# Two mixtures of experts behind a short attention: side work queued behind residues, expert scales folded into factors, and a new rate for layer two's weights

## The chip, the core and the metric

The kernel runs on one core of a Trainium2 chip. The metric is the device time of one execution in microseconds (us). The engines are named as in the profile: PE multiplies matrices (PEld is its loading of weights), DVE and ACT work on whole tiles, POOL issues the gathers and scatters and some small operations, SP issues all other transfers. Each engine takes its instructions in the order of its queue, and an instruction that waits for a semaphore holds up all behind it.

## What is computed

There are N = 7168 tokens of D = 192 numbers. A causal local attention comes first (window K = 7, 8 heads, softmax over the window). Then layer one sends each token to its two best of E = 8 experts, layer two to its best one. An expert is `relu(x @ w1[e]) @ w2[e]` with 1024 hidden numbers.

```python
# layer one
noisy = x @ w_gate + log1p(exp(x @ w_noise)) * noise
top2 = argpartition(-noisy, 2)[:, :2]; g = softmax(noisy at top2)
out[t] = sum over k of g[t, k] * (relu(x[t] @ w1[e]) @ w2[e])      # e = top2[t, k]
# layer two, on the output x of layer one
logits = (x / (norm(x) + 1e-6)) @ (emb / (norm(emb) + 1e-6)).T / tau
out[t] = max(softmax(logits[t])) * (relu(x[t] @ w1[e]) @ w2[e])    # e = argmax
```

## The kernel before

**Tiles.** A list of rows is made for each layer: rows are sorted by expert into tiles of 256 (pairs) and, at the end of a layer's sections, of 128 (singles). Layer one has 56 pairs and 4 singles that always run, layer two 28 and 4; further singles stand in a branch that is seldom taken. The loop over `seq` runs one tile per turn: `first_product` of the next tile (line 1112: 40 products, in four groups; ACT makes the float16 part `hh` of each group, line 1114; DVE makes its residue, line 1115, called `hl` or `wt` by the buffer) is interleaved with `second_product` of this one (line 1138, 48 products), then ACT scales the result (line 1143) and POOL scatters it (line 1146): layer one's to `yb`, layer two's to the output. Rows come by gathers that POOL issues three tiles ahead (line 1062, into `xg`), weights by SP (line 1080, `wb<-ws`), one tile's in two transfers, skipped where the expert is still in the buffer.

**Scaling.** Values are kept as two float16 parts, with powers of two taken out. A row's factor travels with it in column 192 of `xg`; that of an expert is in `cprod`. For each tile DVE multiplies the two into `sc` (line 1123), which ACT applies at line 1143. `scales` (line 742) looks up `cprod` for each place in the order of tiles, into `csl`.

**Side work.** All that makes the lists is done beside the tiles: the attention of token columns 24 to 40 and 40 to 56 (the first 24 come in the head, where no tile runs yet), its logits, choices, ranks and lists s1 and s2 (lists two and three of layer one); then for layer two `combine_gen` (loads `yb`, adds a token's two results with the choice factors `gates`), `post_chunk` (norms, splitting and logits of four columns, a chunk), `choose2`, `gate_gen` (the factor of each row, and the rows themselves), ranks and lists c0, c1, c2; and `prep_gen`, which reads an expert's weights, takes their power of two out, splits them into two float16 parts (`wo`, ACT line 366 and DVE line 368) and writes them to `ws`. Layer one's weights are done in the head, layer two's beside the tiles: eight jobs, 56 pieces at line 368.

These are Python generators that yield their cost in us on DVE (real part) or ACT (imaginary part). `Queue.point` runs at eight points of a pair's turn, six of a single's, and hands out `SHARE` = 0.845 us of credit on each. It runs steps of threads and chains while credit is left, and `P_STEPS` = 0.64 steps of the weights' thread a point. Before the gather of the first tile of a new list, `finish` runs all steps that are left for that list. `yield "lag"` in a generator leaves it until the next point.

**The order.** What a generator emits gets the next priority in the tile framework; the framework's scheduler orders each engine's queue by priority among what it takes to be ready. So an instruction of side work can stand in DVE's queue ahead of a residue that was emitted before it. `tc.issue_after(x.ins)` puts an instruction behind x in the queue of x's engine. `after_product` does so with the last product on PE and is used for side work there; `after_tile` does so with the last residue on DVE (`state["pin"]`) and is used for the taps of the attention alone (line 420).

Of the kernel before, what the change touches and what calls it, by code (L numbers as in the profile page):

```python
# [7 lines left out]
F32 = mybir.dt.float32  # L8
F16 = mybir.dt.float16
BF16 = mybir.dt.bfloat16  # L10
I32 = mybir.dt.int32
AF = mybir.ActivationFunctionType
# [4 lines left out]
NCOL = N // 128  # L17
# [12 lines left out]
R_LOW = 40000  # L30
P_STEPS = 0.64
SHARE = 0.845
# [51 lines left out]
def two_moe(ctx: ExitStack, tc: tile.TileContext, x, wgen, w_gate, w_noise, noise, w1a, w2a, emb, tau, w1b, w2b, out):  # L84
# [35 lines left out]
    def lag(n):  # L120

        for _ in range(0 if head["on"] else n):
            yield "lag"
# [264 lines left out]
    def softmax_gen(a, b):  # L388
        n = (b - a) * H
        w = wt[:, a:b].rearrange("p t h k -> p (t h) k")  # L390
        m = rt.tile([128, GM * H], F32, name="sm_m")
        with (tc.issue_after(state["ctl"].ins) if a == G1[1][0] else ExitStack()):
            V.tensor_reduce(m[:, :n], w, axis=AX.X, op=ALU.max)
        yield 6.0e-3 * n
        V.tensor_tensor(w, w, m[:, :n, None].to_broadcast([128, n, K]), op=ALU.subtract)
        yield 6.0e-3 * n
        A.activation(w, w, AF.Exp)
        yield 0.5
        V.tensor_reduce(m[:, :n], w, axis=AX.X, op=ALU.add)
        V.tensor_scalar(m[:, :n], m[:, :n], 1e-9, None, op0=ALU.add)  # L400
        V.reciprocal(m[:, :n], m[:, :n])
        yield 12.0e-3 * n
        V.tensor_mul(w, w, m[:, :n, None].to_broadcast([128, n, K]))
        yield 6.0e-3 * n
# [48 lines left out]
    sx = consts.tile([128, 2, NCOL], F32, name="sx")  # L453
    isx = consts.tile([128, 2, NCOL], F32, name="isx")
    y_loads = []

    def post_chunk(l, acc, a, lg, g0, rows_i, done, whole=None):
# [5 lines left out]
        for c in range(CH):  # L463
            A.activation(rows_i.bitcast(F16)[:, c, 0:192] if l else xs[:, c], acc[c], AF.Square, accum_out=nrm[:, l, a + c:a + c + 1])
        yield 1.6j
        pow2(nrm[:, l, s].bitcast(I32), sx[:, l, s], isx[:, l, s], CH, 194, 60)
        yield 0.4
# [113 lines left out]
    def gate_gen(g, lg, a, b):  # L581

        n = b - a
        s = rt.tile([128, GM], F32, name="ss")[:, :n]
        with tc.issue_after(state["lg"].ins) if "lg" in state else ExitStack():
            PL.tensor_tensor(s, nrm[:, 1, a:b], half[:, :n], op=ALU.pow)
        yield 0.1
        yield from lag(4)
        V.tensor_scalar(s, s, 1e-6, None, op0=ALU.add)
        V.reciprocal(s, s)  # L590
        V.tensor_scalar(s, s, itau[:, 0:1], None, op0=ALU.mult)
        V.tensor_mul(lg, lg, s[:, :, None].to_broadcast([128, n, E]))
        yield 0.8
        A.activation(lg, lg, AF.Exp)
        yield 0.4
        yield from lag(1)
        V.tensor_reduce(s, lg, axis=AX.X, op=ALU.add)
        V.tensor_scalar(s, s, 1e-9, None, op0=ALU.add)
        V.reciprocal(s, s)
        V.tensor_mul(gate2[:, a:b], s, isx[:, 1, a:b])  # L600
        yield 0.7
        V.tensor_copy(rows2[g][:, :, 192:196].bitcast(F32), gate2[:, a:b, None].to_broadcast([128, b - a, 4]))
        write_rows(1, rows2[g], a, b - a)
        yield 0.2
# [62 lines left out]
    flag_i = [consts.tile([128, len(L.order)], I32, name=f"fi{l}") for l, L in enumerate((L1, L2))]  # L667
    csl = [consts.tile([128, len(L.order)], F32, name=f"csl{l}") for l, L in enumerate((L1, L2))]
    gidx = [consts.tile([128, L.units], I32, name=f"gx{l}") for l, L in enumerate((L1, L2))]
# [71 lines left out]

    def scales(l, a, b):
        while l not in ready:
            yield None
        n = b - a
        e = exec_e[l]
        t = rt.tile([128, 768], F32, name="cmp")[:, 0:64 * E].rearrange("p (a b) -> p a b", b=E)
        V.tensor_tensor(t[:, :n], e[:, a:b, None].to_broadcast([128, n, E]), iof[:, None, 0:8].to_broadcast([128, n, E]),
                        op=ALU.is_equal)
        yield 0.6  # L750
        V.tensor_mul(t[:, :n], t[:, :n], cprod[l][:, None, :].to_broadcast([128, n, E]))
        V.tensor_reduce(csl[l][:, a:b], t[:, :n], axis=AX.X, op=ALU.add)
        yield 0.9

# [85 lines left out]
    def decode(l, v, n, us):  # L840
# [10 lines left out]
        else:  # L851
            vi = rt.tile([128, 128], F32, name="df2").bitcast(I32)
            pv = rt.tile([128, 128], I32, name="dpv")
            V.tensor_copy(vi[:, :n], v)
# [29 lines left out]
    def section_open(l, L, g, key):  # L884
# [32 lines left out]
        def tables():  # L917
            yield from slot_experts(l, s0, s1)
            yield from exec_tables(l, s0, s1)
            yield from scales(l, s0, s1)  # L920

# [37 lines left out]
    def section_last(l, L, key):  # L959
# [30 lines left out]
        def tables():  # L990
# [22 lines left out]
            yield from exec_tables(l, sec, len(L.order))  # L1013
            yield from scales(l, sec, len(L.order))

# [39 lines left out]
    def gather(i):  # L1055
        l, L, pos, u, nh = tiles[i]

        xg = att.tile([128, 1, RW], I32, name="junk", bufs=1) if "rare" in state else work.tile([128, 2, RW], I32, name="xg", bufs=4)
        rows_in = 128 * L.groups[max(g for g in range(len(L.groups)) if pos >= L.first[g])][1]
        live[i] = {"xg": xg}  # L1060
        for h in range(nh):
            PL.indirect_dma_start(out=xg[:, h], out_offset=None, in_=T[l][0:rows_in],  # L1062
                                      in_offset=bass.IndirectOffsetOnAxis(ap=gidx[l][:, u + h:u + h + 1], axis=0))
# [33 lines left out]
    def first_product(i, bg):  # L1097
# [7 lines left out]
        for g in range(4):  # L1105
# [14 lines left out]
            yield  # L1120
        xg = live[i]["xg"]
        sc = work.tile([128, 2], F32, name="sc1", bufs=1) if "rare" in state else work.tile([128, 2], F32, name="sc", bufs=3)
        V.tensor_scalar(sc[:, :nh], xg[:, :nh, 192:193].bitcast(F32).rearrange("p h o -> p (h o)"), csl[l][:, c:c + 1], None, op0=ALU.mult)  # L1123
        live[i] = {"h": (hh, hl), "sc": sc}

    def second_product(i, bg):
        l, L, pos, u, nh = tiles[i]
        _, w = slot(i)
        (hh, hl), sc = live[i]["h"], live[i]["sc"]
        w2 = w[:, 4096:].rearrange("p (f a d) -> p f a d", f=8, a=2)  # L1130
# [11 lines left out]
        for h in range(nh):  # L1142
            A.activation(ys[:, h], py[:, h], AF.Copy, scale=sc[:, h:h + 1])  # L1143
        dst, bound = (YB, 2 * N - 1) if l == 0 else (out, N - 1)
# [38 lines left out]
    def combine_gen(g):  # L1183
        a, b = L2.groups[g]
        while state.get("free", 0) < 1 if g == 0 else 1 not in ready:
            yield None
        nxt = combine_load(a)
        yield from lag(5)
        for c0 in range(a, b, CH):
# [30 lines left out]
    def ctl(l, g, key):  # L1220
# [4 lines left out]
        if l == 0:  # L1225
            yield from choose1(lgs[0][g], a, b)
        else:
            yield from choose2(lgs[1][g], a, b)
            bgq.chain(gate_gen(g, lgs[1][g], a, b), key)
# [4 lines left out]
    class Job:  # L1234
# [4 lines left out]

        def step(self):  # L1240
            if self.rank is None:
                return next(self.g)
# [8 lines left out]
    class Queue:  # L1251
# [29 lines left out]
        def point(self, share):  # L1281
# [5 lines left out]
            for it in list(self.chains):  # L1287
                if min(self.credit.real, self.credit.imag) < -0.6:
                    break
                try:  # L1290
# [8 lines left out]
                    moved = True  # L1299
            self.steps += P_STEPS  # L1300
            while self.steps >= 1.0:
# [153 lines left out]
```

## Time and profile before

| | us |
|---|---|
| median of three runs (1038.93 to 1042.97) | 1039.67 |
| profiled execution | 1037.56 |
| its span, first to last instruction | 1035.8 |

| engine | busy us | share | instructions |
|---|---|---|---|
| PE | 907.2 | 88% | 9714 |
| DVE | 698.4 | 67% | 1852 |
| ACT | 579.9 | 56% | 1247 |
| POOL | 396.5 | 38% | 368 |

The profile is of one execution. Busy shares mix the head (to 145 us, without tiles), the stretch with attention and layer one, the change of layers, and the end, where tiles run without side work; a stretch's limit is read from that stretch. The views used below are the table of busy time by stretch, the chain that ended last in order of time, the waits of an engine by what ended them, single instructions in order of time, and the instructions of one line.

### The profile page before, as it was taken

The numbers are of one execution on the slowest core, as the hardware profiler recorded it, in microseconds if no ns is written. First come the engines' busy times: TensorE is split into PE (matmuls) and PEld (weight loads), VectorE is DVE, ScalarE is ACT, GpSimd is POOL, SyncE is SP. The second block draws the span as 40 slices with busy tenths as digits, with TensorE's granted clock in tenths as the row PEclk, the third lists the DMA queues.
The fourth block names the chain that finished last, engine by engine and source line by source line (L and its number), as shares of the span: only waits on it lengthen the run. The fifth ranks groups of instructions, "written<-read, shape, count | busy, mean of one in ns | idle before, by whom it ended". The sixth has DMA issues, their size and how long they took to land.

```text
span 1035.8 us, 26302 instructions
## 1 busy us (share of the span) xinstructions
PE 907.2 (88%) x9714; PEld 824.9 (80%) x9714; DVE 698.4 (67%) x1852; ACT 579.9 (56%) x1247; POOL 396.5 (38%) x368
## 2 busy tenths in 40 slices
PE   4894159999998899799998989879998999999995
PEld 2452138988897798699997879869988999999995
DVE  7897988999998788965357667385757763333331
ACT  2879635567565767455565854265447444444442
POOL 1000053565245453316443535344435354444422
PEclk9997569999999999999998989999999999999998
DMA  8687873766469486546989959674576835777650
GB/s 270 194 271 228 294 271 107 255 185 198 132 213 348 156 265 229 167 178 209 323 312 334 358 196 320 207 250 147 182 260 215 295 121 185 262 262 265 220 219 22
DMA packets 96395, 236.34 MB, mean 228 GB/s; under 512 B 13439, under 2 KB 64223, under 8 KB 87808
## 3 DMA queue, kind: packets, MB, share of 16 engines
q1 hardware_dynamic: 79360, 200.35, 56.7%
q0 software_dynamic: 16896, 34.20, 10.8%
q8 instruction: 79, 1.29, 0.5%
q14 instruction: 60, 0.49, 0.1%
HBM read 230.60 MB, written 57.90 MB: 279 GB/s over the span
## 4 chain that ended last, share of the span: by engine, by line
PE 51%; DVE 21%; DMA 10%; issue 6%; ACT 6%; POOL 3%; SPq 1%; POOLq 0%; DVEq 0%; ACTq 0%
PE ph L1112 23%; PE py L1138 20%; DVE tmp L420 3%; DMA wb<-ws 3%; PE py L447 2%; DVE wo L368 2%; DVE hl L1115 2%; DVE wt L1115 2%; DVE acc L435 2%; DMA xg<-t,gx 2%; DMA tmp<-yb 2%; PE pt L1090 2%; ACT wo L366 1%; PE rb L503 1%; POOL xg L1062 1%
## 5 line engine op out<-in xcount | busy, mean ns | idle before, releaser
L1112 PE MATMUL ph<-xt,wb 128*128 128x256 f16 x3360 | 421.8, 278 | 37.8 <-DVE hl L1115 17.0
L1112 PEld LDWEIGHTS <-wb 128*128 128x128 f16 x3360 | 330.4, 100 | 81.9 <-issue 27.8
L1138 PE MATMUL py<-wb,hh 128*128 128x192 f16 x2688 | 354.9, 247 | 0.0
L1114 ACT ACTIVATE hh<-ph 128x512 f16<-128x512 f32 (+1 forms) x368 | 210.3, 577 | 232.3 <-PE ph L1112 218.1
L1062 POOL DMA_INDIRECT xg<-t,gx x176 | 191.3, 1087 | 343.6 <-DVE gx L849 133.0
L1138 PEld LDWEIGHTS <-hh 128*128 128x128 f16 x2816 | 253.9, 98 | 3.8
L1146 POOL DMA_INDIRECT yb<-ys,sx x116 | 128.6, 1109 | 186.8 <-ACT ys L1143 161.2
L1115 DVE SCALAR_TENSOR_TENSOR wt<-ph,hh 128x512 f16<-128x512 f32 x184 | 125.9, 687 | 100.3 <-ACT hh L1114 100.0
L1138 PE MATMUL py<-wb,wt 128*128 128x192 f16 x736 | 181.5, 247 | 0.0
L1115 DVE SCALAR_TENSOR_TENSOR hl<-ph,hh 128x512 f16<-128x512 f32 (+1 forms) x184 | 117.4, 641 | 84.1 <-ACT hh L1114 81.8
L1138 PE MATMUL py<-wb,hl 128*128 128x192 f16 x608 | 149.8, 246 | 0.0
L1143 ACT ACTIVATE ys<-py,sc 128x192 f32<-128x192 f32 x176 | 64.6, 416 | 89.5 <-PE py L1138 76.5
L1146 POOL DMA_INDIRECT out_dram<-ys,sx x60 | 61.3, 1021 | 94.0 <-ACT ys L1143 80.0
L420 DVE TENSOR_TENSOR tmp<-xh,wt 128x768 f32<-128x768 f32 x90 | 84.5, 950 | 2.9 <-PE ph L447 1.5
L1138 PEld LDWEIGHTS <-wt 128*128 128x128 f16 x736 | 72.2, 98 | 0.1
L1092 ACT ACTIVATE xt<-pt 128x768 f16<-128x768 f16 x84 | 67.9, 808 | 4.4 <-PE pt L1090 4.3
L1138 PEld LDWEIGHTS <-hl 128*128 128x128 f16 x672 | 66.1, 98 | 0.1
L1123 DVE TENSOR_SCALAR sc<-xg,csl 128x2 f32<-128x2 f32 (+1 forms) x92 | 21.2, 233 | 57.7 <-ACT ys L1143 53.0
L366 ACT ACTIVATE wo<-xh,wsc 128x384 f16<-128x384 f32 (+1 forms) x76 | 45.9, 659 | 16.0 <-DVE wsc L261 15.8
L1090 PE MATMUL pt<-identh,xg 128*128 128x128 f16 x528 | 45.8, 222 | 8.4 <-DMA xg<-t,gx 8.4
L368 DVE SCALAR_TENSOR_TENSOR wo<-xh,wsc,wo 128x384 f16<-128x384 f32 (+1 forms) x76 | 48.9, 675 | 3.3 <-ACT wo L366 3.2
L447 PE MATMUL py<-tmp,ident 128*128 128x384 f32 x84 | 33.9, 554 | 15.2 <-DVE tmp L420 13.7
(323 smaller groups left out, 990.2 us busy)
## 6 DMA issues: line engine op xcount, KB each, us to landing
wb<-ws SPq DMA_DIRECT2D x84, 1024.0 KB
wb<-ws SPq DMA_DIRECT2D x84, 768.0 KB
ws<-wo SPq DMA_DIRECT2D x16, 768.0 KB
tmp<-yb SPq DMA_DIRECT2D x28, 384.0 KB
ws<-wo SPq DMA_DIRECT2D x16, 512.0 KB
ws<-wo SPq DMA_DIRECT2D x32, 256.0 KB
xh<-ws SPq DMA_DIRECT2D x8, 1024.0 KB
xh<-in_moe_w_dram SPq DMA_DIRECT2D x10, 768.0 KB
```

The lines of the kernel that those rows point to most:

```text
L366: A.activation(h, v, AF.Copy, scale=sc[:, c:c + 1])
L368: V.scalar_tensor_tensor(lo, v, sc[:, c:c + 1], h, op0=ALU.mult, op1=ALU.subtract)
L420: V.tensor_mul(dst.rearrange("p t (h g) -> p (t h) g", g=G), xv, w)
L1062: PL.indirect_dma_start(out=xg[:, h], out_offset=None, in_=T[l][0:rows_in], in_offset=bass.IndirectOffsetOnAxis(ap=gidx[l][:, u + h:u + h ...
L1090: PE.transpose(pt[:, j, h], xg[:, h, 128 * b:128 * b + 128], identh)
L1092: A.activation(xt.rearrange("p j h n -> p (j h n)"), pt.rearrange("p j h n -> p (j h n)"), AF.Copy)
L1112: state["pe"] = mark = PE.matmul(ph[:, q, :n], s, m, start=j == 0, stop=j == 4)
L1114: A.activation(hh[:, fs, :n], ph[:, :, :n], AF.Relu)
L1115: state["pin"] = V.scalar_tensor_tensor(hl[:, fs, :n], ph[:, :, :n], 0.0, hh[:, fs, :n], op0=ALU.max, op1=ALU.subtract)
L1138: state["pe"] = PE.matmul(py[:, h], t[:, f, hs], w2[:, f, c], start=f == 0 and j == 0, stop=f == 7 and j == 2)
L1143: A.activation(ys[:, h], py[:, h], AF.Copy, scale=sc[:, h:h + 1])
L1146: d = PL.indirect_dma_start(out=dst, out_offset=bass.IndirectOffsetOnAxis(ap=sidx[l][:, u + h:u + h + 1], axis=0), in_=ys[:, h], in_offset ...
```

## The change

- Every step of side work, once tiles run, is put behind the last residue in DVE's queue (`Job.step`).
- `sc` and `csl` go. Layer one: `fold_gen` multiplies `gates` by the expert's scale, once, after list three's choice, by the one-hot choices `oh`; `combine_gen` waits for it. Layer two: `gate_gen` multiplies its factor by the expert's scale before the rows are written; it waits until layer two's weights are done. ACT scales with the column of `xg`, which lives until then and has five buffers instead of four.
- `P_STEPS` is 0.35 until list s2 is done, 1.0 from there on.
- The power 0.5 of layer two's norms is taken on POOL per chunk in `post_chunk`, not per group in `gate_gen`; the lag before it is used goes.
- The lag between `combine_gen`'s first loads and their use is 14 points instead of 5.
- Two scratch tiles share the memory of others (`sm_m`, `dpv`).

```diff
 R_LOW = 40000
-P_STEPS = 0.64
+P_STEPS = (0.35, 1.0)
 SHARE = 0.845
...
         w = wt[:, a:b].rearrange("p t h k -> p (t h) k")
-        m = rt.tile([128, GM * H], F32, name="sm_m")
+        m = ranks[1][0].rearrange("p e c -> p (e c)")
         with (tc.issue_after(state["ctl"].ins) if a == G1[1][0] else ExitStack()):
...
     isx = consts.tile([128, 2, NCOL], F32, name="isx")
+    root = consts.tile([128, NCOL], F32, name="root")
     y_loads = []
...
         yield 1.6j
+        if l:
+            PL.tensor_tensor(root[:, s], nrm[:, 1, s], half[:, :CH], op=ALU.pow)
         pow2(nrm[:, l, s].bitcast(I32), sx[:, l, s], isx[:, l, s], CH, 194, 60)
...
         s = rt.tile([128, GM], F32, name="ss")[:, :n]
-        with tc.issue_after(state["lg"].ins) if "lg" in state else ExitStack():
-            PL.tensor_tensor(s, nrm[:, 1, a:b], half[:, :n], op=ALU.pow)
-        yield 0.1
-        yield from lag(4)
-        V.tensor_scalar(s, s, 1e-6, None, op0=ALU.add)
+        V.tensor_scalar(s, root[:, a:b], 1e-6, None, op0=ALU.add)
         V.reciprocal(s, s)
...
         yield 0.7
+        while 1 not in ready:
+            yield None
+        c = expert_scale(1, 0, a, b)
+        V.tensor_mul(gate2[:, a:b], gate2[:, a:b], c)
+        yield 0.8
         V.tensor_copy(rows2[g][:, :, 192:196].bitcast(F32), gate2[:, a:b, None].to_broadcast([128, b - a, 4]))
...
     flag_i = [consts.tile([128, len(L.order)], I32, name=f"fi{l}") for l, L in enumerate((L1, L2))]
-    csl = [consts.tile([128, len(L.order)], F32, name=f"csl{l}") for l, L in enumerate((L1, L2))]
     gidx = [consts.tile([128, L.units], I32, name=f"gx{l}") for l, L in enumerate((L1, L2))]
...
-    def scales(l, a, b):
-        while l not in ready:
+    def expert_scale(l, k, a, b):
+
+        n = b - a
+        t = rt.tile([128, 768], F32, name="cmp")[:, 0:n * E].rearrange("p (a b) -> p a b", b=E)
+        c = rt.tile([128, NCOL], F32, name="xsc")[:, :n]
+        V.tensor_mul(t, oh[l][k][:, a:b], cprod[l][:, None, :].to_broadcast([128, n, E]))
+        V.tensor_reduce(c, t, axis=AX.X, op=ALU.add)
+        return c
+
+    def fold_gen():
+
+        while 0 not in ready:
             yield None
-        n = b - a
-        e = exec_e[l]
-        t = rt.tile([128, 768], F32, name="cmp")[:, 0:64 * E].rearrange("p (a b) -> p a b", b=E)
-        V.tensor_tensor(t[:, :n], e[:, a:b, None].to_broadcast([128, n, E]), iof[:, None, 0:8].to_broadcast([128, n, E]),
-                        op=ALU.is_equal)
-        yield 0.6
-        V.tensor_mul(t[:, :n], t[:, :n], cprod[l][:, None, :].to_broadcast([128, n, E]))
-        V.tensor_reduce(csl[l][:, a:b], t[:, :n], axis=AX.X, op=ALU.add)
-        yield 0.9
+        for k in range(2):
+            c = expert_scale(0, k, 0, NCOL)
+            yield 1.2
+            V.tensor_mul(gates[:, k], gates[:, k], c)
+            yield 0.2
+        state["folded"] = True
...
             vi = rt.tile([128, 128], F32, name="df2").bitcast(I32)
-            pv = rt.tile([128, 128], I32, name="dpv")
+            pv = rt.tile([128, 128], I32, name="dv")
             V.tensor_copy(vi[:, :n], v)
...
             yield from exec_tables(l, s0, s1)
-            yield from scales(l, s0, s1)
...
             yield from exec_tables(l, sec, len(L.order))
-            yield from scales(l, sec, len(L.order))
...
-        xg = att.tile([128, 1, RW], I32, name="junk", bufs=1) if "rare" in state else work.tile([128, 2, RW], I32, name="xg", bufs=4)
+        xg = att.tile([128, 1, RW], I32, name="junk", bufs=1) if "rare" in state else work.tile([128, 2, RW], I32, name="xg", bufs=5)
         rows_in = 128 * L.groups[max(g for g in range(len(L.groups)) if pos >= L.first[g])][1]
...
             yield
-        xg = live[i]["xg"]
-        sc = work.tile([128, 2], F32, name="sc1", bufs=1) if "rare" in state else work.tile([128, 2], F32, name="sc", bufs=3)
-        V.tensor_scalar(sc[:, :nh], xg[:, :nh, 192:193].bitcast(F32).rearrange("p h o -> p (h o)"), csl[l][:, c:c + 1], None, op0=ALU.mult)
-        live[i] = {"h": (hh, hl), "sc": sc}
+        live[i]["h"] = (hh, hl)
...
         _, w = slot(i)
-        (hh, hl), sc = live[i]["h"], live[i]["sc"]
+        (hh, hl), xg = live[i]["h"], live[i]["xg"]
         w2 = w[:, 4096:].rearrange("p (f a d) -> p f a d", f=8, a=2)
...
         for h in range(nh):
-            A.activation(ys[:, h], py[:, h], AF.Copy, scale=sc[:, h:h + 1])
+            A.activation(ys[:, h], py[:, h], AF.Copy, scale=xg[:, h, 192:193].bitcast(F32))
         dst, bound = (YB, 2 * N - 1) if l == 0 else (out, N - 1)
...
         a, b = L2.groups[g]
-        while state.get("free", 0) < 1 if g == 0 else 1 not in ready:
+        while "folded" not in state or (state.get("free", 0) < 1 if g == 0 else 1 not in ready):
             yield None
         nxt = combine_load(a)
-        yield from lag(5)
+        yield from lag(14)
         for c0 in range(a, b, CH):
...
             yield from choose1(lgs[0][g], a, b)
+            if g == len(L.groups) - 1:
+                bgq.chain(fold_gen(), "c0")
         else:
...
         def step(self):
+            with after_tile() if not head["on"] else ExitStack():
+                return self.run()
+
+        def run(self):
             if self.rank is None:
...
                     moved = True
-            self.steps += P_STEPS
+            self.steps += P_STEPS[ctl_done.get("s2", False)]
             while self.steps >= 1.0:
...
                 if self.threads[2]:

```

## Rows read from the trace of the kernel before

**Rows 1.** Table by stretch: length, busy us (instructions) by engine, PE clock, DMA share, GB/s.
```profile
144.90:443.70 298.80, 272.95 (x2987) 252.54 (x2987) 264.67 (x667) 187.06 (x399) 135.47 (x116) 0.97 0.65 208
443.70:711.70 268.00, 247.15 (x2782) 230.52 (x2780) 155.81 (x413) 149.57 (x338) 115.70 (x104) 0.95 0.76 262
711.70:847.60 135.90, 130.78 (x1515) 123.60 (x1513) 92.98 (x329) 68.69 (x146) 61.12 (x56) 1.00 0.64 214
```

**Rows 2.** The same table for line 1112 alone: PE busy, PEld busy.
```profile
144.85:443.70 298.85, 147.24 (x1160) 114.28 (x1160) 0.97 0.65 208
711.70:847.55 135.85, 68.34 (x560) 53.92 (x561) 1.00 0.64 214
```

**Rows 3.** Chain that ended last, in order: start us, length us, what.
```profile
282.44 1.10 PE rb L813 x8
...
802.05 2.18 PE ph L1112 x20
...
811.89 2.18 PE ph L1112 x20
...
856.43 2.18 PE ph L1112 x20
...
865.10 2.18 PE ph L1112 x20
```

**Rows 4.** PE's waits, 145 to 444: us in total, times, longest.
```profile
PE ph L1112 <- DVE hl L1115: 12.8, 11, 6.4
PE ph L1112 <- DMA wb<-ws: 6.3, 2, 4.9
PE ph L1112 <- DVE lg L520: 3.1, 1, 3.1
```

**Rows 5.** PE's waits, 444 to 711.
```profile
PE rb L503 <- DVE lg L520: 9.0, 2, 4.9
PE ph L1112 <- DMA wb<-ws: 4.0, 1, 4.0
```

**Rows 6.** PE's waits, 711 to 850.
```profile
PE rb L503 <- DVE lg L520: 2.2, 2, 2.0
```

**Rows 7.** Waits over the whole span.
```profile
DVE tmp L1193 <- DMA tmp<-yb: 16.4, 4, 5.5
...
DVE ss L589 <- POOL ss L586: 8.1, 3, 3.0
```

**Rows 8.** PE in order of time: start, length, instruction, [idle before, releaser].
```profile
438.68 1.65 PE L1112 MATMUL ph<-xt,wb 128*128 128x256 f16 x7 [6.42 <-DVE hl L1115]
```

**Rows 9.** DVE in order of time, the same stretch.
```profile
433.96 0.96 DVE L877 TENSOR_TENSOR cmp<-iof,lu 128x768 f32<-128x768 f32 x1
...
437.94 1.28 DVE L1115 SCALAR_TENSOR_TENSOR hl<-ph,hh 128x512 f16<-128x512 f32 x2
```

**Rows 10.** Line 813, 440 to 480: ns min/median/max, first and last start, forms.
```profile
L813 PE MATMUL rb<-orr,ol x32: 291/312/320, 450.4 to 462.0; 128*128 128x70 bf16 x32
```

**Rows 11.** Line 1123 over the whole span, the same columns.
```profile
L1123 DVE TENSOR_SCALAR sc<-xg,csl x92: 205/228/368, 146.1 to 1003.3; 128x2 f32<-128x2 f32 x84, 128x1 f32<-128x1 f32 x8
```

**Rows 12.** Line 368 by stretch: DVE busy (pieces), PE clock, DMA share, GB/s.
```profile
260.00:440.00 180.00, 16.48 (x23) 0.97 0.68 217
440.00:622.00 182.00, 18.26 (x32) 0.95 0.78 273
500.00:590.00 90.00, 4.49 (x8) 0.94 0.95 339
```

**Rows 13.** Loads of weights on the chain that ended last.
```profile
238.31 5.14 DMA wb<-ws
...
328.23 11.66 DMA wb<-ws
```

**Rows 14.** The power on POOL, lines 586 and 247.
```profile
L586 POOL TENSOR_TENSOR ss<-nrm,half x3: 3095/3168/4259, 590.8 to 788.9; 128x16 f32<-128x16 f32 x2, 128x24 f32<-128x24 f32 x1
...
L247 POOL TENSOR_TENSOR nr<-nr,half x1: 1669/1669/1669, 379.8 to 379.8; 128x8 f32<-128x8 f32 x1
```

## The prediction

> **What bounds the kernel now.** The page's busy shares say little, as they mix stages, so I read the table by stage first [rows 1]. I call 144.9 to 443.7 us stage A, 443.7 to 711.7 stage B, 711.7 to 847.6 stage C. What comes before is the head, what comes after is a tail in which nothing of the change runs but the scaling at a tile's end. The second table counts the products of line 1112 in A and C [rows 2]: a tile has 40 of them, so 29 pair tiles start in A and 14 in C.
>
> The chain in order of time gives the pace of an undisturbed pair tile: 865.10 - 856.43 = 8.67 us; a tile that also carries one chunk's logits takes 811.89 - 802.05 = 9.84, so a chunk costs PE 1.2 us, and eight products of a list take 1.10 [rows 3]. Stage A at that pace: 29 x 8.67 = 251.4, eight chunks 9.4, list two with its four times eight products 4.4: 265 of 298.8 us. So A loses some 33 us. C at that pace: 14 x 8.67 = 121.4, four chunks 4.7, two shorter lists 4.4: 130.5 of 135.9, a loss of 5. B has singles in it, so I take its loss from named waits alone. Who ended PE's waits is the next view: in A the residues on DVE (hl, 12.8 us), weight loads (6.3) and logits on DVE (lg, 3.1) [rows 4]; in B logits 9.0 and weights 4.0 [rows 5]; in C logits 2.2 [rows 6]. So PE bounds the body, and DVE, which is 264.7 of 298.8 us busy in A [rows 1], is the engine that makes it late.
>
> DVE works in queue order, so what stops it stops the residues too. Three times it waits for the power on POOL (8.1 us in all, 3.0 the longest) and four times for the loads of yb (16.4 in all) [rows 7].
>
> **Side work behind residues.** The largest single wait shows what this edit is about. PE stops for 6.42 us until a residue ends [rows 8]; until 437.94 DVE was busy with the list's leftovers (line 877 at 433.96 and its neighbours, 0.96 us each), and then does two residues in a row, 1.28 us [rows 9]. That side work was no help to its own chain: the list's products on PE, which it feeds, run from 450.4 to 462.0 [rows 10], since PE's side work is already queued behind emitted products. After the edit a residue that is emitted first goes first. At stake in A are 12.8 + 3.1 = 15.9 us of PE's waits. Not all can go: after all edits DVE still has to do about 250 us there (below) beside PE's 265. Bounds 0 and 15.9; I take 8, half, as the 6.42 us wait has an excess of side work right before it, and the ten others, with a mean of 0.6 us, may be met again in another place. In B and C residues are rarely late, 0 here. A cost below nothing: while PE waits for weights, pinned side work can't fill the gap. The wait for weights is 6.3 us in A and 4.0 in B [rows 4, 5], and side work that is moved by so much makes a later chain late by at most that; I put 2 us against the gain.
>
> **Scales folded.** Each tile loses one DVE instruction of 0.23 us, 92 in all = 21 us, of which 29 x 0.23 = 6.7 lie in A [rows 11]. Six calls of `scales` go, three operations each. `fold_gen` adds two products and two sums over 448 elements and two small products, `gate_gen` three operations on at most 192 elements for each group; an operation on 768 elements takes 0.96 us [rows 9], so the fold costs at most 4, and each gate at most 2 us, about what `scales` took. They run after list three, where DVE is 155.8 of 268.0 us busy [rows 1]. The scaling on ACT reads the rows' own column instead: the same instruction. The rows must then live until that scaling, hence a fifth buffer; nothing is late by it, as the freed slot is that of an earlier tile. `gate_gen` now waits for layer two's weights before it writes rows: its last piece comes by 622 us [rows 12] and no later than now (next part), while layer two's first gathers belong to the first tiles of C. Without the DVE time that it gives in A this edit is worth 0 (DVE has room in B, C and the tail); that part is in the 250 above.
>
> **Layer two's weights.** The rate falls from 0.64 to 0.35 steps a point until list three, then rises to 1.0; a pair tile has eight points. Line 368 runs once for each of layer two's 56 pieces: 23 from 260 to 440, where list three ends, 32 from there to 622 [rows 12]. So some 24 of 56 are done when list three is; at 0.35/0.64 of the rate it is 13. That takes 11 x 16.48/23 = 7.9 us off DVE before list three, and the other 43 pieces at 1.0/0.64 = 1.56 times the old pace take (622 - 440) x (43/32)/1.56 = 157 us instead of 182: done no later. DVE in A: 264.7 - 6.7 - 7.9 = 250. Step costs are charged to the same credit as the lists, so lists two and three end a tile or so earlier and less of them is forced ahead of their gathers. I take 3 us for it, bounds 0 and 6.
>
> Against it stands DMA: 56 pieces stand for some 27 MB read and written; from 500 to 590, where the mean share is already 0.95 at 339 GB/s [rows 12], 8 pieces become some 12 to 14, or 2 to 3 MB more, which at 339 GB/s is 6 to 9 us of transfers, with 0.05 x 90 = 4.5 us of room. I take 3 us against, bounds 0 and 9. A weight load in a calm stretch takes 5.14 us, one behind prep's loads and stores 11.66 [rows 13]: that is how a queue ahead of weights is paid.
>
> The page DMA: Bandwidth & Descriptors (Trainium skill), section Queues, rings and completion order, says that descriptors of one queue are consumed in ring order on each DMA engine. By that rule stores that SP issues first are passed first, and all of the 6 to 9 us would be PE's, the third rival below; the long load agrees with it, but the forecast doesn't need it.
>
> **Power per chunk, and the longer lag.** The power leaves `gate_gen`; DVE's 8.1 us of waits for it go [rows 7]. POOL gets 14 instructions, one for each chunk of layer two, instead of 3. For 8 elements it took 1.67 us, for 16 3.10 to 3.17, for 24 4.26 [rows 14]: about 0.18 an element, so 4 elements cost some 0.95, bounds 0.7 and 1.67, and 14 of them 13 us instead of 10.5. POOL is 115.7 of 268.0 us busy in B [rows 1]: hidden, while its gathers run three tiles ahead; without that cover 14 x 1.67 = 23 would be the end.
>
> GPSIMD Engine Reference (Trainium skill), section Instruction dispatch, says that every instruction pays a software dispatch, which speaks against splitting one. By the line through the sizes the fixed part here is 0.2 us, which would be 11 x 0.2 = 2 us of POOL, and nothing of the sum changes.
>
> The lag of 14 points instead of 5 gives the loads 9 more points, more than a tile; the longest wait was 5.5 us [rows 7], so all 16.4 go. Of these 24.5 us on DVE, PE saw part: logits late by 9.0 in B and 2.2 in C [rows 5, 6]. I take 11.2 - 3 (side work that stays) = 8, bounds 3 and 14. Layer two's third list is emitted a tile later; it has the distance of the gathers, three tiles, for cover.
>
> **The sum.** Residues -8 + 2, lists -3, DMA +3, power and lag -8: -14 us. The profiled execution took 1037.56 us with a span of 1035.8, 2.1 us under the median of 1039.67. 1037.6 - 14 = 1023.6 for an execution like it; beside the median 1025.7. I say 1024.
>
> **Rivals.** First, **bigger**: with all upper bounds (15.9, 6, 14, no loss) it is 1037.6 - 36 = 1002; half way to there 1012. For it: waits of A and B have one cause, a full DVE queue, and the granted clock is 0.95 in B but 1.00 in C [rows 1], so that a stall also makes later products slow. Against: in A DVE stays 94% as loaded as PE (250 of 265).
>
> Second, **no gain**: residues come in time, but transposes and logits, whose DVE work now queues behind residues, come later by the same amount; PE's waits change their name from hl to rows and lg. Gain of residues 0, of lists 0, loss 2 and 3, power and lag -3 to -8: 1035 to 1040. For it: lg already ends 9.0 us of waits in B [rows 5].
>
> Third, **slower**: the 500 to 590 stretch is bound by DMA. It decides once the room there (4.5 us) is used up by prep's extra megabytes: at the end of its bounds, +9 us of late weights, and as much again where the clock falls after each stall and stays low for the products behind it (B as a whole has 0.95 against 1.00 in C [rows 1]). With half the gains elsewhere (-7): 1037.6 + 18 - 7 = 1048.
>
> Fourth, the change doesn't do what it says: the scheduler keeps side work behind residues but pulls residues themselves late. That is the second case in effect, with its time.
>
> **Chances.** Forecast 0.58, with a range of its own from 1013 to 1034; bigger 0.14; no gain 0.17; slower 0.11. A measurement here can tell about 0.5%, 5.2 us, from no change. Faster by more than that (under 1034.5): forecast and bigger, 0.73 with a little from either side. Within: 0.16. Slower: 0.11. The range of 8 in 10 leaves out the slower case and the best part of the bigger one: 1005 to 1040.
>
> **What would show it.** Right: around list three no wait for hl over 2 us, and side work right after residues on DVE; no DVE wait for POOL or for the loads of yb; 15 to 18 of the 56 pieces of weights before list three; A shorter by 8 to 12 us, B by 3 to 8. Wrong: waits for weights in 500 to 590 that add up to more than 8 us (third), or PE's waits for rows and lg that grow by what hl loses (second). A time above 1034 would mean that residues were late because DVE was full and not because of its order.

## The result and the profile after

| | before | after |
|---|---|---|
| median, us (four runs each, same chip) | 1040.12 | 1029.21 |
| ratio, 95% interval | | 0.9884 [0.987, 0.9899] |
| profiled execution, us | 1037.56 | 1030.61 |
| its span, us | 1035.8 | 1028.8 |

The changed kernel is 10.9 us faster by the medians. Its profiled execution happened to be the longest of its four, so the two traces differ by only 7.0 us of span. A second execution of the changed kernel (e9, below) splits its time otherwise, with 289.5 us in A and 271.5 in B, so the length of one stage in one trace is good to some 4 us. Line numbers moved: the first product is now line 1120, its residues are line 1123, the loads of weights line 1088, the combination of `yb` line 1198, a list's products line 823; line 368 stayed.

The table by stretch of the changed kernel, cut at the same tiles as [rows 1] (tile 29 starts at 429.7, tile 56 at 705.4, tile 70 at 839.7; the last row is tiles 29 to 38). Columns: PE, PEld, DVE, ACT, POOL busy, PE clock, DMA share, GB/s.

```profile
144.40:429.70 285.30, 270.76 (x2996) 252.69 (x2996) 249.66 (x604) 169.21 (x364) 133.11 (x114) 0.98 0.60 191
429.70:705.40 275.70, 242.14 (x2689) 225.34 (x2688) 154.71 (x388) 158.36 (x353) 111.83 (x108) 0.94 0.81 277
705.40:839.70 134.30, 132.30 (x1582) 124.95 (x1581) 95.00 (x314) 76.21 (x166) 67.68 (x62) 1.00 0.68 225
429.70:520.50 90.80, 80.60 (x845) 75.31 (x844) 42.02 (x90) 51.59 (x101) 34.11 (x35) 0.92 0.69 236
```

Stage A went from 298.8 to 285.3 us, B from 268.0 to 275.7, C from 135.9 to 134.3; the head gives 0.5 and the tail takes 0.9. So A brings 13.5 us and B gives 7.7 of it back (9.3 and 3.5 in e9). All of that loss lies in tiles 29 to 38, which took 77.9 us before and take 90.8 now; the rest of B is 5.2 us shorter.

PE's waits in A of the changed kernel (us in total, times, longest), against [rows 4]:

```profile
PE rb L823 <- DVE orr L833: 3.1, 2, 1.8
...
PE ph L1120 <- DVE hl L1123: 2.5, 4, 0.9
...
PE rb L641 <- DVE th L635: 1.9, 1, 1.9
```

Residues end 2.5 us of waits where they ended 12.8. No wait is put down to weights (6.3 before), but the wait of 2.5 us at 155 us that this trace puts down to nothing ("issue") is a load of weights in e9 (3.8). The lists' own DVE work is now what PE waits for now and then.

One line of [rows 4] was read wrongly: the 3.1 us that `lg` ends. That product reads no logits; it also waits for a load of weights that was issued at 309.57 us and landed at 315.82, 0.04 us before PE went on, and in e4 the trace names that load for the same wait. So weights ended 9.4 us of waits in A before, and what residues ended was 12.8 us by `hl` and, left out in [rows 4], 2.2 by `wt`. The waits in B, 429.7 to 705.4, against [rows 5]:

```profile
PE ph L1120 <- DMA wb<-ws: 9.8, 3, 6.5
PE ph L1120 <- DMA xh<-ws: 7.0, 2, 6.4
PE ph L1120 <- PEq L1379: 6.7, 1, 6.7
PE ph L1120 <- DVE hl L1123: 5.2, 2, 4.5
PE ph L1120 <- ACT junk L320: 3.8, 1, 3.8
PE rb L506 <- DVE lg L523: 0.5, 1, 0.5
```

Logits fell from 9.0 to 0.5 us, but loads of weights rose from 5.3 (`wb` 4.0 and `xh` 1.3 in B before) to 16.8. The 3.8 us put to the squares on ACT (`junk`) belong to them too: the product reads nothing of the squares, it also waits for a load that was issued at 469.68 us and landed at 479.47, 0.04 us before PE went on, and e9 names the load (4.0 us at 483.82). So it is 20.6 us, as in e9. `PEq L1379` is the branch to the tiles that are seldom taken, 2.2 us before (`DVEq`). And where [rows 7] has DVE stopped for 16.4 us by the loads of `yb` and for 8.1 by the power on POOL, the whole span now has one line for the first and none for the second:

```profile
DVE tmp L1198 <- DMA tmp<-yb: 0.4, 2, 0.2
```

### The profile page after: what moved, and what is told of

The parts are those of the page before. It is cut to its first block, busy times and chain, and to the rows that moved or that the text cites. A ratio compares the mean times of both kernels' runs of the same rounds, so it can differ in the third digit from the quotient of the medians.

```text
span 1028.8 us, 26128 instructions
## 1 busy us (share of the span) xinstructions
PE 903.4 (88%) x9714; PEld 822.6 (80%) x9714; DVE 687.5 (67%) x1757; ACT 578.8 (56%) x1247; POOL 400.0 (39%) x379
## 5 line engine op out<-in xcount | busy, mean ns | idle before, releaser
L1070 POOL DMA_INDIRECT xg<-t,gx x176 | 183.7, 1044 | 188.5 <-DVE gx L859 132.2
L1151 POOL DMA_INDIRECT yb<-ys,sx x116 | 132.0, 1138 | 273.6 <-ACT ys L1148 253.9
L1148 ACT ACTIVATE ys<-py,xg 128x192 f32<-128x192 f32 x176 | 64.9, 416 | 86.1 <-PE py L1143 78.5
L320 ACT ACTIVATE junk<-xh 128x768 f16<-128x768 f32 (+1 forms) x38 | 35.8, 943 | 25.3 <-DMA xh<-in_moe_w_dram 24.9
```

The costliest lines, as they stand in the source:

```text
L1148: A.activation(ys[:, h], py[:, h], AF.Copy, scale=xg[:, h, 192:193].bitcast(F32))
L1151: d = PL.indirect_dma_start(out=dst, out_offset=bass.IndirectOffsetOnAxis(ap=sidx[l][:, u + h:u + h + 1], axis=0), in_=ys[:, h], in_offset ...
```

## The experiments

Each edit starts from the kernel that is named. All ratios are against the kernel before, run on the same chip.

**e1_unpinned**: the changed kernel without the order behind residues.

```diff
         def step(self):
-            with after_tile() if not head["on"] else ExitStack():
-                return self.run()
+            return self.run()
```

> The changed kernel with side work no longer queued behind residues; all else as after (1029 us). First theory: the order on DVE is what made stage A shorter (in the changed kernel the 34th tile starts 15.8 us earlier than before), so that gain falls to 3 to 6 us and the time is 1036 to 1044. Rival 1: the lower rate and the lighter DVE made it, the order did not: 1027 to 1031. Rival 2: the order also causes the loss of about 14 us from 466 to 515 us, because stores of prep wait on SP for pieces that are queued behind residues: that loss goes with it, and 1025 to 1033 may come out with stage A slow and that stretch fast.

1027.62 us, 0.9854 [0.9787, 0.992]: no slower than the changed kernel, whose ratios are 0.9884 and 0.9879 (e9). So at the new rates no gain of the order is seen. Stage A took 283.4 us. The theory that the order had made A short falls. DVE's waits came back, though:

```profile
DVE tmp L1198 <- DMA tmp<-yb: 14.1, 4, 7.8
...
DVE ss L588 <- POOL root L468: 5.7, 3, 4.0
```

**e2_pin_alone**: the kernel before with that order and nothing else.

```diff
         def step(self):
+            with after_tile() if not head["on"] else ExitStack():
+                return self.run()
+
+        def run(self):
```

> The kernel before with the queueing behind residues alone. First theory: stage A 8 to 12 us shorter and no loss behind it, 1028 to 1033 us. Rival 1 (the order does nothing, the lighter DVE did it): 1038 to 1042. Rival 2 (the order makes prep's stores late on SP): stage A shorter, but 5 us or more lost between list three and 620 us, 1034 to 1040.

1036.31 us, 0.9939 [0.9909, 0.9969], or -6.2 us. But A is 301.5 us, not shorter, and B 264.4, 3.6 shorter; the span of its trace is 1035.0, only 0.8 under that of before, so where the 6.2 us lie isn't seen in it. PE's waits in A:

```profile
PE rb L517 <- ACT xt L509: 6.0, 2, 3.3
PE ph L1112 <- DVE hl L1115: 5.3, 6, 1.2
PE pt L1090 <- DMA xg<-t,gx: 3.8, 2, 2.8
PE ph L1112 <- DMA wb<-ws: 3.4, 2, 1.9
```

The order does what it says: the longest wait for a residue falls from 6.4 to 1.2 us. What it frees in A is taken by other waits, chiefly of the logits' transposes and of gathers, as the second rival of the prediction has it.

**e3_rate_flat**: the changed kernel with the old rate.

```diff
-P_STEPS = (0.35, 1.0)
+P_STEPS = (0.64, 0.64)
```

> The changed kernel with the rate of layer two's weights at 0.64 throughout, as before. First theory: the rate of 1.0 puts too many bytes and waits of ACT for loads into 466 to 515 us and costs some 12 us there, while the 0.35 gave stage A 3 to 4: 1018 to 1023. Rival 2 (pinned pieces hold SP's queue, at any rate): the loss between 466 and 620 us stays, 1028 to 1034.

1021.75 us, 0.9798 [0.9724, 0.9872]: faster than the changed kernel. A is 296.4 us, B 255.3. So, with the order in place, the low rate is what shortens A, and the high rate costs B more.

**e4_power_lag**: the kernel before with the power per chunk and the longer lag (and `pv` in the tile `dv`).

```diff
+            PL.tensor_tensor(root[:, s], nrm[:, 1, s], half[:, :CH], op=ALU.pow)
...
-        yield from lag(5)
+        yield from lag(14)
```

> The kernel before with the power per chunk and the lag of 14 alone. First theory: DVE's waits for POOL and for the loads of yb are gone and PE gets 5 to 8 us of it, in stages B and C alone: 1032 to 1036. Rival: PE waits by the same amount for later logits: 1038 to 1041.

1033.16 us, 0.9893 [0.982, 0.9965]: -9.4 us by the medians, -11 by the ratio, with a wide interval. DVE's waits hardly moved:

```profile
DVE tmp L1192 <- DMA tmp<-yb: 14.7, 4, 5.1
...
DVE ss L588 <- POOL root L468: 6.3, 3, 4.3
```

Yet no wait of PE for logits is left after 430 us, where [rows 5, 6] have 11.2.

The next four ran on a chip whose runs can't be set beside the others: PE has many short gaps there that the trace puts down to nothing ("issue"). In the one kernel that was traced on both kinds of chip, the scales folded alone, these are the waits of that form on `py`:

```profile
PE py L1144 <- issue: 9.8, 24, 1.0
```

On the other chip the same kernel has no such line, and was 1039.13 us (e12, below) against 1064.03 here. So I use the waits of these four, and no ratios.

**e5_rate_alone**: the kernel before with the two rates alone.

```diff
-P_STEPS = 0.64
+P_STEPS = (0.35, 1.0)
...
-            self.steps += P_STEPS
+            self.steps += P_STEPS[ctl_done.get("s2", False)]
```

> The kernel before with the rates 0.35 and 1.0 alone. New theory: the low rate, not the order, made stage A shorter, as it takes prep's transfers out of the way of the tiles' weights; the high rate gives that back in stage B. So the 33rd tile starts 10 to 17 us earlier than before and the end is within 6 us of before: 1034 to 1042. Rival: the low rate needs the order or the folded scales to work (stage A gains under 5 us), 1040 to 1050.

1052.11 us, 1.0052 [1.002, 1.0084], over the range of the theory. The 33rd tile starts 9 us earlier than before (464.9 us), short of its 10 to 17. In A PE waits 0.5 us for weights. In 444 to 730 us the waits for `wb` add up to 23.1 us, with one of 12.8.

**e6_fold_alone**: the kernel before with the scales folded into the factors, and the scratch tiles shared as in the change.

```diff
-            A.activation(ys[:, h], py[:, h], AF.Copy, scale=sc[:, h:h + 1])
+            A.activation(ys[:, h], py[:, h], AF.Copy, scale=xg[:, h, 192:193].bitcast(F32))
...
+            V.tensor_mul(gates[:, k], gates[:, k], c)
...
+        V.tensor_mul(gate2[:, a:b], gate2[:, a:b], c)
```

> The kernel before with the folded scales alone (and their shared scratch tiles). First theory: 21 us of DVE instructions go, 7 of them in stage A, and PE sees 0 to 4 us of it: 1036 to 1041. Rival: the instruction that waits for ACT at each tile's end held up residues in the full stage A, so its loss gives 5 to 9 us: 1031 to 1035. Rival: rows that live longer make gathers late: 1042 or more.

1064.03 us, 1.0179 [1.0129, 1.0229]; this turned out to be the chip, as e12 shows.

**e7_rate_35_75**: the changed kernel with a lower second rate.

```diff
-P_STEPS = (0.35, 1.0)
+P_STEPS = (0.35, 0.75)
```

> The changed kernel with rates 0.35 and 0.75 in place of 0.35 and 1.0. If the rate in stage B is what gives the 16 us of stage A back, half to all of it is kept: 1012 to 1022. If layer two's weights then come too late for its lists, layers change with a stall and it is 1026 to 1035.

1056.52 us, 1.0096 [1.006, 1.0131]: with 16.1 us of waits for weights in B, this tells nothing on a rate between the two.

**e8_flat_pool_stores**: the changed kernel at 0.64 throughout, with layer two's prepared weights stored from POOL's queue and not SP's.

```diff
-                        SP.dma_start(WS[l][1][(e + c) * 128:(e + c + 1) * 128], wo)
+                        (PL if l else SP).dma_start(WS[l][1][(e + c) * 128:(e + c + 1) * 128], wo)
```

(and the same in lines 374 and 378)

> The changed kernel at a rate of 0.64 throughout, with layer two's stores to ws issued by POOL instead of SP: same bytes, but SP no longer waits for pieces of wo ahead of weight loads. If SP's order makes weights late, PE's waits for weights in stage A fall from 15.7 us (at this rate, stores on SP) to under 5 and the time is 1008 to 1016. If the bytes make them late, 12 us or more of these waits stay and it is 1019 to 1026. If POOL's gathers are held up by the stores, PE waits for gathers and it is over 1028.

1059.41 us, 1.0119 [1.0056, 1.0182], so the time settles nothing. But of the waits for weights in A (15.7 us in e3, which has the same rate and order) one is left:

```profile
PE pt L1098 <- DMA xg<-t,gx: 4.1, 2, 2.9
...
PE ph L1120 <- DMA wb<-ws: 0.3, 1, 0.3
```

The same bytes move, at the same rate; only the queue that the stores stand in differs. (Both traces have one more wait at the start of A, put down to nothing: 3.2 us here, 3.6 in e3.) The gathers, which are issued from POOL, pay something for it (4.1 us, against 2.0 in e3).

The four below ran on one chip, with none of those gaps on `py`.

**e9_changed_again**: the changed kernel, no edit.

> The changed kernel once more, on one chip with the next three, as the four runs before (rate alone, folded scales alone, 0.35/0.75, stores on POOL) were on a chip where PE had 8 to 18 us of gaps that nothing in the profile ends and that no other trace has. Ratio to before 0.987 to 0.990 as on the first chip; if ratios depend on the chip, it is over 0.995 and the four runs say nothing against the first chip's.

1026.61 us, 0.9879 [0.9844, 0.9913]: as at first.

**e10_flat_again**: e3 once more.

> The changed kernel at the rate 0.64 throughout, again, beside the changed kernel on one chip. If the rates cost what the two traces say (stage A gives 16 us, the stretch to 620 us takes them back and more), it is 4 to 10 us faster than the changed kernel. If that was the chip, within 3 us of it.

1018.21 us, 0.9796 [0.9765, 0.9826]. It beats both kernels: 22 us under before, 8.4 under the changed one. A and B of it:

```profile
144.20:440.90 296.70, 270.79 (x2986) 251.28 (x2985) 254.63 (x618) 185.88 (x396) 135.63 (x118) 0.97 0.65 210
440.90:695.50 254.60, 240.01 (x2717) 224.01 (x2718) 155.32 (x385) 145.39 (x327) 109.43 (x105) 0.96 0.78 274
```

A is hardly shorter than before, B is shorter by 13.4 us. PE waits for weights in A (145 to 444 us) rather than for residues:

```profile
PE ph L1120 <- DMA wb<-ws: 19.4, 6, 6.2
...
PE ph L1120 <- DVE hl L1123: 0.3, 1, 0.3
```

**e11_flat_unpinned**: both edits, the old rate and no order behind residues; what is left of the change is the folded scales, the power per chunk and the lag.

> The changed kernel at the rate 0.64 and without the queueing behind residues: folded scales, power per chunk and lag alone. If the order gives something of its own, as it did alone (1036.3 beside 1042.5 us), it is 4 to 10 us slower than the run at 0.64 with the order. If the order is worth nothing once the other edits are in, as in the run without it at the rates 0.35 and 1.0, it is within 3 us of it.

1024.55 us, 0.9857 [0.983, 0.9884]. A 290.3 us, B 262.3. So at the old rate the order brings 6.3 us (its interval and that of e10 don't touch): it costs 6.4 in A and gives 7.7 in B by the traces, whose spans differ by 2.6 only.

**e12_fold_again**: e6 once more.

> The folded scales alone, again, on another chip. If the 1.018 of the first time was that chip's gaps, the ratio is 0.99 to 1.00 here. If the folded scales really cost time without the power per chunk and the lag (a wait for POOL that now stands in another place, rows that live longer), it is over 1.01 again, and the waits for logits in stage B show it.

1039.13 us, 0.9983 [0.9961, 1.0006]: within the noise.

## Why the prediction was right, and where not

The sum held: -14 us predicted, -10.9 measured (-13.8 in e9), faster and within the range. Its terms did not. From the last chip's medians, without anything taken from the first term to the last: folded scales, power and lag 1040.36 to 1024.55, -15.8; the order at the old rate -6.3; the new rate in that kernel +8.4. Predicted were -8, -6 and 0. The sum came out by luck: one term was nearly 8 us too small, another 8 too hopeful. The split depends on the path, too: at the new rates no gain of the order is seen (e1), so by that path the rates cost nothing and the order +2.6 by the ratios, within the intervals.

**Residues: size right at the old rate alone, place wrong.** I forecast -8 + 2 in stage A. The order measured -6.2 (e2) and -6.3 (e10 against e11) at the old rate and none at the new ones (e1), and no trace has a gain of it in A, which is 2.7 and 6.4 us longer with it. The wait of 6.42 us that the term rests on goes without the order as well: `hl` ends 3.8 us of waits in A with the folded scales alone (e12) and 3.7 in e11, 1.2 the longest. So the order isn't needed for that; e4, which leaves DVE's work in A as it was, keeps the wait (6.4). What should show it right did come: around list three no wait for `hl` is over 0.9 us, and DVE does a residue as soon as there is one, with the list between. DVE of the changed kernel in order of time:

```profile
421.36 0.68 DVE L1123 SCALAR_TENSOR_TENSOR hl<-ph,hh 128x512 f16<-128x512 f32 x1
421.96 0.17 DVE L804 CAST rwi<-rwk 128x32 int32<-128x32 f32 x1
...
422.34 0.68 DVE L1123 SCALAR_TENSOR_TENSOR hl<-ph,hh 128x512 f16<-128x512 f32 x1
...
424.24 0.45 DVE L833 TENSOR_TENSOR orr<-ou,vtab 128x560 bf16<-128x560 bf16 x1
424.60 0.69 DVE L1123 SCALAR_TENSOR_TENSOR hl<-ph,hh 128x512 f16<-128x512 f32 x1
```

Compare [rows 9], where the residues came after the side work. The step that failed is "side work that is moved by so much makes a later chain late by at most that; 2 us": I named the waits for weights as a gap that pinned work can't fill, and didn't ask what waits for the pinned work. Layer two's weights are side work too. Their pieces (line 368) now come one behind each residue, and SP, which stores them, waits for each with the loads of weights behind it. At the old rate waits for weights in A rise from 9.6 us without the order (e11) to 19.4 with it (e10; 4.0 of it is the wait at the start of A, which e3 puts down to nothing, and e3 has 15.7).

**Low rate: mechanism right, size too small.** Predicted 13 pieces before list three ends, 3 us. (The 15 to 18 of the sign didn't follow from the working.) Line 368 over 145 to 430 us, and from there on:

```profile
L368 DVE SCALAR_TENSOR_TENSOR wo<-xh,wsc,wo x12: 737/742/747, 292.3 to 414.4; 128x512 f16<-128x512 f32 x12
...
L368 DVE SCALAR_TENSOR_TENSOR wo<-xh,wsc,wo x44: 605/611/744, 449.6 to 638.0; 128x384 f16<-128x384 f32 x32, 128x512 f16<-128x512 f32 x12
```

Twelve, then. DVE's work in A came out as worked out (249.7 us against 250) as a sum. List three's products end at 435.1 us, where they ended at 462.0 [rows 10]: 27 us, not "a tile or so"; the rate alone brings 18 of it (433.2 in e1, 451.1 in e11) to 20 (439.3 in e9, 459.4 in e10). In A the low rate is worth 7 us with the order (289.5 in e9 against 296.7 in e10) and 7 without (283.4 in e1 against 290.3 in e11): it takes half of prep's stores and loads out of A, which I hadn't counted, and the waits for weights in A go to 3.8 us (e9) and 0 (e1). DVE itself got only 4.8 and 3.6 us lighter by it (254.6 to 249.8, 255.0 to 251.4), not 7.9.

**High rate: the term that was mis-sized.** I gave it 3 us, bounds 0 and 9, by the megabytes in 500 to 590 us, and "done no later" was the step that failed. By the working the last piece would have come 157 us after list three, at some 597 us; before it came at 607.5, now it comes at 638.0. In 500 to 590 us 21 pieces run, not 12 to 14, because I spread the old pace evenly: before, 23 pieces lie between 440 and 530, and in 500 to 590 only the 8 of [rows 12]. B costs 17 us more than at the old rate with the order (271.5 against 254.6) and 13 without (275.1 against 262.3).

By the sign that I had set, waits for weights in 500 to 590 over 8 us, the third rival's loss is there: 6.5 and 7.0. (The sign tells little: e10, the fastest kernel, has 9.0 there.) The two long waits of tiles 29 to 38, 3.80 and 6.40 us, make 10.2 of their 12.9 us; the rest is PE's slower work behind them, with a granted clock of 0.50, the lower of its two levels, at 478.1 to 484.9 and 502.0 to 508.8 us, as that rival has it, but less than it took. Its cause, prep's bytes, fits the first wait: SP issued two loads of raw weights at 465.23 and 466.95 us, which landed at 473.56 and 476.44, and the tile's load at 469.68, which landed at 479.47, with DMA busy all the while (380 GB/s in 469.7 to 479.5 us). It doesn't fit the second, before which DMA has a share of 0.46, at 164 GB/s, in 481 to 491 us. There SP waits.

SP's waits in 440 to 640 us of the changed kernel, where before no wait for `wo` stands:

```profile
SPq L372 <- DVE wo L368: 36.8, 6, 12.1
SPq L374 <- DVE wo L368: 15.4, 4, 4.9
...
SPq L378 <- DVE wo L368: 5.2, 2, 4.6
```

That is 57 us; 26.0 at the old rate with the order (e10), 22.2 at the new one without (e1), 3.7 with neither (e11). How it reaches PE is seen at 482 to 506 us, in the second wait: on DVE each piece stands behind a residue; on SP, in order, a store follows its piece, and the load of weights follows the stores; then comes PE's wait. Three engines of the changed kernel, one after the other:

```profile
482.50 0.69 DVE L1123 SCALAR_TENSOR_TENSOR hl<-ph,hh 128x512 f16<-128x512 f32 x1 [5.89 <-ACT hh L1122]
483.10 0.74 DVE L368 SCALAR_TENSOR_TENSOR wo<-xh,wsc,wo 128x512 f16<-128x512 f32 x1
...
485.24 0.74 DVE L368 SCALAR_TENSOR_TENSOR wo<-xh,wsc,wo 128x512 f16<-128x512 f32 x1
...
489.64 0.69 DVE L1123 SCALAR_TENSOR_TENSOR hl<-ph,hh 128x512 f16<-128x512 f32 x1 [1.07 <-ACT hh L1122]
490.25 0.74 DVE L368 SCALAR_TENSOR_TENSOR wo<-xh,wsc,wo 128x512 f16<-128x512 f32 x1
```

```profile
486.04 0.35 SPq L374 DMA_DIRECT2D ws<-wo  x1
491.05 3.13 SPq L378 DMA_DIRECT2D ws<-wo  x4
494.22 1.05 SPq L307 DMA_DIRECT2D xh<-in_moe_w_dram  x1
497.74 0.35 SPq L1088 DMA_DIRECT2D xh<-ws  x1
```

```profile
479.51 2.74 PE L1120 MATMUL ph<-xt,wb 128*128 128x256 f16 x12 [3.80 <-ACT junk L320]
...
505.85 1.25 PE L1120 MATMUL ph<-xt,xh 128*128 128x128 f16 x10 [6.40 <-DMA xh<-ws]
```

DVE was idle for 5.89 us ahead of 482.50 with a piece queued behind the residue; the residue waited for PE, and PE for its weights (the first wait, which this trace puts to ACT). The piece at 485.24 frees the store at 486.04, for which SP had waited 4.9 us, and that at 490.25 the stores at 491.05, after 4.6 us more. The load goes out at 497.74, 17.0 us after the load of weights before it (480.73), and PE has its weights at 505.85. Without the order (e11) pieces run in twos and threes when their input is there:

```profile
483.43 1.15 DVE L368 SCALAR_TENSOR_TENSOR wo<-xh,wsc,wo 128x384 f16<-128x384 f32 x2 [0.51 <-ACT wo L366]
484.49 0.69 DVE L1123 SCALAR_TENSOR_TENSOR hl<-ph,hh 128x512 f16<-128x512 f32 x1
...
486.22 1.67 DVE L368 SCALAR_TENSOR_TENSOR wo<-xh,wsc,wo 128x384 f16<-128x384 f32 x3
```

The page DMA: Bandwidth & Descriptors (Trainium skill), section Queues, rings and completion order, which the prediction set beside this term, speaks of descriptors that are in a ring already. The first wait agrees with it, as the three loads above landed in the order of their issue; in the second the load isn't issued yet, so SP's rows decide and not that rule.

Shown is this chain once, in the trace, and, for A, that waits for weights go when the stores leave SP (e8). That B would get its time back in that way isn't shown, since e8's chip left its time open. Nor is the part of DMA's bytes in the loss after 540 us: e1, with the same rate, loses 1.3 us in tiles 29 to 38 (79.2 us, against 77.9 before), but its tiles 38 to 56 take 195.8 us against 184.4 in e11. Late weights don't make that difference: they end 11.6 us of waits in B of e1 and 14.2 in e11 (with 7.6 that its trace puts to `xh` of line 465 on ACT, where a load landed 0.04 us before); e1 has 5.9 at the branch and 4.7 for layer two's first list on DVE instead. Whether the new rate costs anything at all without the order stays open as well: the medians of e1 and e11 have one ratio, on two chips, while the profiled executions differ by 7.4 us.

**Power and lag: PE's gain right, DVE's path wrong.** I let all 24.5 us of DVE's waits go, and PE gain 8 by it. PE's waits for logits after 430 us did go: 11.2 before, 12.3 with the folded scales alone (e12), 4.8 with the order alone (e2), none in e4, 0.6 in e11 and 0.7 in e10. The time agrees: -9.4 (e4, by the medians), or -15.8 with the folded scales (e11), above the 8 that I took and around the bound of 14. But DVE's waits stayed in all kernels without the order: 14.7 and 6.3 in e4, 13.4 and 5.3 in e11. With the order and the old lag 13.0 is left for `yb` and nothing for the power (e2); with order and lag 0.4. My step "9 more points, so all 16.4 go" took the point of emission for the place in the queue; that the scheduler puts what it takes to be ready further ahead fits the runs, since the order brings the place back, but no run shows the scheduler at it. So PE's gain doesn't need those waits to go; which of the two edits takes away PE's waits for logits wasn't tried. On POOL the power took longer than forecast, hidden as forecast:

```profile
L468 POOL TENSOR_TENSOR root<-nrm,half x14: 1007/1116/1839, 566.1 to 803.1; 128x4 f32<-128x4 f32 x14
```

That is 15.6 us by the median, where I had 13.

**Folded scales: 0, as said.** 0.9983 [0.9961, 1.0006].

**The rivals.** "No gain" fell for the whole change: waits for rows and logits did not take the place of `hl`; for the order alone it is what stage A shows (e2). "Bigger" (1012) was reached by no kernel; e10, the change at the old rate, comes nearest with 1018.21. "Slower" came true in part of B, by late weights and a lower clock, and was outweighed. For the fourth, residues pulled late, nothing speaks: the one long wait for a residue in B, 4.5 us until 586.6, is 5.0 us in e1 without the order, and its `hh` had stood behind side work on ACT.

## What to carry to other kernels

Before work is pinned behind something on one engine, list who waits for that work on other queues: here a store on SP waits for a pinned piece, and loads that PE needs stand behind the store. With such an order in place, a rate for background transfers was better kept even here; slowing it in one stage (-7 us) and catching up in the next (+17) cost 8.4. Before a wait is put to the engine that a trace names, check that the instruction reads something of it: three waits here were loads of weights that landed 0.04 us before. When parts push in both directions, measure each alone and in pairs on one chip: a sum that comes out right says little about its terms.

## What was unexpected of the hardware

One chip showed gaps on PE that no event in the trace ends, 24 on `py` alone in one execution, 1.0 us at most each, and the kernel before ran at 1047.43 us there against 1040.36 and 1042.52 on others. The gaps don't account for all of the difference: the folded scales alone took 24.9 us more there than elsewhere, with 16.6 us of waits marked "issue". A ratio against the same kernel on the same chip didn't correct for it (1.0179 there, 0.9983 here).
